# An FFT filter with two feed-forward layers on one core: weight lower parts formed by TensorE, the gate's half moved into the gain, the last inverse stage in fp32r

## The chip, the cores and the metric

The kernel runs on one core of one Trainium2 chip. The metric is the device time of one execution in microseconds (us), the median of several runs. One core has TensorE (PE, with its weight loads shown apart as PEld), VectorE (DVE), ScalarE (ACT), GpSimd (POOL) and SyncE (SP), and 16 DMA engines. All transfers but the early filter's stores are issued from SP's queue.

## The reference, cut to what matters

Sizes: batch 8, sequence 3072, width 256, so 24576 rows of 256; first layer 1024 wide, second 2048 wide.

```python
X = np.fft.rfft(x, axis=1)
Y = X * (filt_r + 1j * filt_i)[None]
x = np.fft.irfft(Y, n=3072, axis=1).reshape(24576, 256)

h = x @ w_in                                  # 256 -> 1024
solu = h * softmax(h)
ln = (solu - mean) / sqrt(var + 1e-6) * g_ln
x2 = ln @ w_out                               # 1024 -> 256

h = x2 @ w_in2                                # 256 -> 2048
g = h * (1 / (1 + exp(-1.702 * h)))
out = g @ w_out2                              # 2048 -> 256
```

The weights arrive as 8-byte floating-point words, and the kernel makes float32 values of them on the chip.

## The kernel before, in words

**Precision.** PE multiplies in two ways here. Operands of type fp32 go in whole, and the profile shows each such matmul as two records of weight load and matmul. Operands of type fp32r are split by the kernel into an upper part (`hi`, an ACT copy that rounds to fp32r) and a lower part (`lo`, a DVE or POOL subtraction), and a product is three matmuls: hi by hi, lo by hi, hi by lo (`product`, and the `terms` lists). Each fp32r matmul is one weight load and one matmul record.

**The filter.** The transform of 3072 points is done as 128 by 24. `step1` multiplies by the 128x128 matrix `fwd1` (fp32 for the first `direct` steps, else three fp32r terms), the result goes to `a_d` in device memory, 32 groups are transformed, weighted and transformed back (`forward`, `weigh`, `inverse`), and `store_z` puts them into `z_d`. Batch 0 is done alone by `EarlyFilter`, then batches 1 and 2 (`ahead`, `dense`), 3 and 4, and so on beside the layers.

**The layers.** There are 96 pairs of 128 rows. For each, class `First` loads `zr` from `z_d`, does the last inverse stage `y` (line 664): four combinations of a half of the width `c` and a piece `cut` of 128 rows, each one fp32 matmul with 128 weight columns out of `zr` and 128 moving columns out of `inv1`. Its result is split into `xh` and `xl`; then come `hidden`, the soft maximum and the normalization (`top` to `norm`), a transposition through device memory (`shuffle`, `gather`, `turn`), and `project`, whose sum `x2` is put into a tile with the tag `zr` (line 777) and split into `x2s`. Class `Second` takes two pairs at a time: 16 steps of `hidden` (line 839), `tanh`, `gate`, `split_hi`, `split_lo` and `output` (line 878), then `finish` (a DVE transposition into `ob`) and `store`. The tag `zr` has one buffer, which the load of `zr` and the sum `x2` use in turn.

**The weights.** Class `Weights` converts 24 parts of 128x512 words. Each goes through `magnitude` (ACT), `clamp`, `shift`, `sign`, `exponent`, `lower` and `add` (six DVE operations: lines 316, 322, 329, 334, 338, 343), `scale_rows` (ACT: the gain `g_ln` into `w_out`, or 0.5 into `w_out2`, line 352), `split_hi` (ACT, line 368) and `split_lo` (DVE, line 371). Parts 0 to 7 in the order of work are the first layer's, 8 to 23 the second layer's.

**Order.** The order on each engine is written out by hand: every step is entered with a due time (`at`), and the instructions are issued in the order of these times. One unit of the time is about 2.2 us in the steady part; a pair has 16 units. The tables `FIRST`, `SECOND`, `FILTER`, `DENSE` and `EARLY` hold the offsets. Each engine, and SP's queue, works through its own list in that order and waits where an operand isn't there.

```python
def product(out, w, x):
    for m, (i, j) in enumerate(((0, 0), (1, 0), (0, 1))):
        nc.tensor.matmul(out, w[i], x[j], start=m == 0, stop=m == 2)
```

Of the kernel before, what the change touches and what calls it, by code (L numbers as in the profile page):

```python
# [39 lines left out]
    "load": -19.18,  # L40
    "y": -15.41,
    "y_lo": -14.98,
    "hidden": ((-13.6, -11.48), (-3.67, -3.45)),
    "top": (-10.45, -2.27),
    "exp": (-9.62, -2.21),
    "weigh": (-8.86, -1.1),
    "square": (-8.1, 0.3),
    "norm": (-6.71, 0.45),
    "shuffle": (-6.64, 1.09),
    "gather": (-4.79, 2.67),  # L50
    "turn": (-1.22, 6.89),
    "u_hi": (-1.02, 7.3),
    "u_lo": (-0.4, 7.44),
    "project": ((9.08, 10.02), (11.05, 11.52)),
    "x2_add": (10.24, 12.96),
    "x2_hi": 13.25,
    "x2_lo": 13.63,
# [4 lines left out]
    "gate": 1.19,  # L62
    "split_hi": 2.49,
    "split_lo": 3.19,
    "output": 4.92,
    "finish": 5.15,
    "store": 6.9,
# [4 lines left out]
    "slots": (-0.44, 3.27, 3.36, 15.01),  # L72
    "first": (-5.28, -2.04, 0.2, 0.75),
    "second": (-4.86, -3.09, -2.5, 0.32, 1.88, 9.31, 12.49, 15.49, 15.68),
# [4 lines left out]
    "start": 15.65,  # L79
    "slots": (0.78, 4.28, 8.58, 12.36),  # L80
    "second": (-6.7, -3.27, -2.21, -0.12, 0.47, 5.53, 7.59, 10.86, 11.01),
# [6 lines left out]
    "end": -36.99,  # L88
    "step1": 25.97,
    "step2": 0.83,  # L90
    "gap": 6.0,
    "x": (-8.35, 0.03),
    "gt": (4.66, 5.2, -4.45),
    "first": (-1.3, -0.46, 5.21),
    "second": (-0.4, 0.64, 1.73, 1.99, 2.68, 3.25, 3.99, 4.34, 4.91),
    "more": (-2.73, -1.19, 0.91, 1.34),
    "direct": 20,
    "between": 0,
    "ahead": ((-20.99, -0.21), (1.01, 1.32)),
    "opening": (-0.05, 2.9),  # L100
    "shift": (-2.49, -2.3, -0.12),
    "loads": (-63.46, -85.07, -66.92, -63.78, -40.07, -39.95, -38.89, -39.87, -38.15, -36.42, -35.26, -29.67, -30.46, -26.83, -28.61, -26.9, -23.26, -23.0, -19.51, -21.51, -16.67, -16.56, -10.11, -9.34),
    "convert": (-61.36, -57.05, -48.5, -52.08, -39.08, -37.53, -36.03, -34.35, -33.55, -30.14, -29.23, -26.36, -27.59, -24.72, -22.78, -21.43, -19.42, -15.97, -16.78, -14.99, -11.07, -11.7, -6.6, -7.06),
    "weight": (-0.98, -0.23, 0.17, 0.46, 0.65, 1.06, 1.27, 1.37, 1.79, 2.41),
    "small": (-44.22, -37.8),
# [24 lines left out]
def dft_constants():  # L130
# [63 lines left out]
    dft1 = np.concatenate([fwd1, inv1], 1)  # L194
# [4 lines left out]
def fft_filter_solu_gelu(  # L199
# [42 lines left out]
    dma(out=dft1_sb, in_=dft1.rearrange("p (t n) -> p t n", t=2))  # L242
# [3 lines left out]
    inv1 = dft1_sb[:, 1]  # L246
# [7 lines left out]
    def load_gain(b):  # L254
        part, rows = blocks(g_ln, b)
        dma(out=g_sb[part], in_=rows.rearrange("(k f) -> f k", f=Q))

# [19 lines left out]
    class Weights:  # L277


        def __init__(self, n, dst, src, gain, k0, kn, c0, cn):  # L280
            self.dst = dst, slice(k0, k0 + kn), slice(c0, c0 + cn)
            self.shape = [P, kn, cn]
            k, c = slice(k0, k0 + kn), slice(c0, c0 + cn)
            self.half = dst is w4
# [34 lines left out]
        def shift(self):  # L319
            self.mag = p2.tile([P, 512], I32, tag="th", name="w_mag")  # L320
            self.f = self.mag.bitcast(F32)
            nc.vector.tensor_scalar(
                out=self.mag, in0=self.wt, scalar1=3, scalar2=0x3FFFFFFF,
                op0=ALU.logical_shift_left, op1=ALU.bitwise_and)

        def sign(self):

            self.top = p2.tile([P, 512], I32, tag="gh", name="w_top")
            nc.vector.scalar_tensor_tensor(
                out=self.top, in0=self.high, scalar=-0x40000000, in1=self.mag,  # L330
                op0=ALU.bitwise_and, op1=ALU.bitwise_or)
# [5 lines left out]
        def lower(self):  # L337
            nc.vector.scalar_tensor_tensor(
                out=self.f, in0=self.low, scalar=2.0 ** -52, in1=self.power,
                op0=ALU.mult, op1=ALU.mult)  # L340

        def add(self):
            nc.vector.tensor_tensor(self.f, self.f, self.top.bitcast(F32), op=ALU.add)
            self.f = self.f.rearrange("p (k n) -> p k n", k=self.shape[1])

        def scale_rows(self):
            if self.half:

                f, self.f = self.f, self.top.bitcast(F32).rearrange(
                    "p (k n) -> p k n", k=self.shape[1])  # L350
                for k in range(self.shape[1]):
# [4 lines left out]
            elif self.gain is not None:  # L356
                for k in range(self.shape[1]):
                    g = self.gain[:, self.k0 + k:self.k0 + k + 1]
                    nc.scalar.activation(
                        out=self.f[:, k], in_=self.f[:, k], func=AF.Copy, scale=g)  # L360

        def split_hi(self):
            dst, k, c = self.dst
            if not dst:
                t = p1.tile([P, 2, K2, D], F32R, tag="w4", name="w4")
                dst.extend(t[:, i] for i in range(2))
            self.hi, self.lo = (t[:, k, c] for t in dst)
            nc.scalar.copy(out=self.hi, in_=self.f)

        def split_lo(self):  # L370
            nc.vector.tensor_tensor(self.lo, self.f, self.hi, op=ALU.subtract)
# [277 lines left out]
    class First:  # L649
        def __init__(self, n):  # L650
            self.n = n
            self.h, self.e, self.v, self.e_d, self.ut, self.x2 = {}, {}, {}, {}, {}, {}

        def load(self):
            b, q = divmod(self.n, NPAIR)
            assert filtered[b] == NG
            self.cuts = segments(q * 2 * P, 2 * P)
            q0, q1 = self.cuts[0][0], self.cuts[-1][0] + 1
            self.zr = p1.tile([N1, 2, D], F32, tag="zr", name="zr")
# [30 lines left out]
        def top(self, a):  # L690
            nmx = p3.tile([P, 1], F32, tag="nmx", name="nmx")
# [3 lines left out]
        def exp(self, a):  # L695
            e = p2.tile([P, FF1], F32, tag="e", name="e")
            se = p3.tile([P, 1], F32, tag="se", name="se")
# [3 lines left out]
            q = p3.tile([P, 1], F32, tag="q", name="q")  # L701
# [5 lines left out]
        def weigh(self, a):  # L707

            e, q = self.e[a], self.v[a]
            su = p3.tile([P, 1], F32, tag="su", name="su")  # L710
            nc.vector.scalar_tensor_tensor(  # L711
                out=e, in0=self.h[a], scalar=1.0, in1=e, op0=ALU.mult, op1=ALU.mult, accum_out=su)
            nmu = p3.tile([P, 1], F32, tag="nmu", name="nmu")
# [4 lines left out]
        def square(self, a):  # L718
            e, (q, nmu) = self.e[a], self.v[a]
            ssq = p3.tile([P, 1], F32, tag="ssq", name="ssq")  # L720
# [4 lines left out]
            rs = p3.tile([P, 1], F32, tag="rs", name="rs")  # L725
# [65 lines left out]
    def plan_first(n):  # L791
# [6 lines left out]
        for a in range(2):  # L798
            in_order(
                v["load"], v["y"], v["y_lo"], *v["hidden"][a],  # L800
                *(v[step.__name__][a] for step in steps), *blocks, v["x2_add"][1], v["x2_hi"], v["x2_lo"], 14.0)
        at(r + v["load"], o.load)
        at(r + v["y"], o.y)
# [14 lines left out]
    class Second:  # L818
# [47 lines left out]
        def output(self, d):  # L866
# [6 lines left out]
            for j in range(self.nf):  # L873
                f = self.nf * d + j
                for h in range(2):
                    for m, (ww, gg) in enumerate(terms):
                        o = self.o[:, h] if self.nf == 1 else self.o[:, h, 0]
                        nc.tensor.matmul(  # L878
                            o, ww[:, f, h * P:(h + 1) * P], self.part(gg, j),
                            start=(f == 0 and m == 0), stop=(f == K2 - 1 and m == 2))  # L880

        def finish(self):

            self.ob = []
            for i in range(len(self.block)):
                pool, tag = ((p1, "ob"), (p2, "xs"))[i]
# [66 lines left out]
    for batches in together[2:]:  # L953
# [9 lines left out]
        plan_filter(batches, lambda i: [piece(i - 4) + d for d in FILTER["first"]], second)  # L963
    for w in weight_parts():
        i = w.n
        t = v["convert"][i]
        steps = (
            w.magnitude, w.clamp, w.shift, w.sign, w.exponent, w.lower, w.add, w.scale_rows,
            w.split_hi, w.split_lo)
        in_order(v["loads"][i], t + v["weight"][0])  # L970
        at(v["loads"][i], w.load)
        in_order(*v["weight"])
        for d, step in zip(v["weight"], steps, strict=True):
            at(t + d, step)
# [43 lines left out]
```

## Time and profile before

| | |
|---|---|
| median of 3 runs | 3665.89 us (3664.22 to 3667.66) |
| the profiled execution | 3660.58 us, span from first to last instruction 3658.7 us |
| mean granted TensorE clock | 0.986 |
| PE busy | 3564.5 us, 97% of the span |
| DVE, ACT, POOL busy | 75%, 56%, 23% |
| DMA | 434.90 MB, mean 119 GB/s |

A row of a group of instructions gives line, engine, operation, names of what is written and read, rows*columns of the weights and the shape of the moving operand, the count, then busy time in us, the mean of one in ns, and the idle time of the engine before it with what ended it. The granted clock is 1.00 at 2.4 GHz and 0.5 at 1.2 GHz. Matmuls are pipelined: a matmul's length holds the way through the array too, so what one costs in a row of many is the distance between starts and not the length.

### The profile page before, as it was taken

To read this page: it belongs to the slowest core of one execution; us is meant where nothing else is said; L and a number is where in the kernel's file an instruction comes from. 1 tells how busy PE (TensorE), PEld (TensorE's weight loads), DVE (VectorE), ACT (ScalarE), POOL (GpSimd) and SP (SyncE) were. 2 spreads that over 40 slices of the span, in tenths; PEclk is the share of its full clock that TensorE was granted. 3 is DMA by queue.
4 is the path that set the end of the run, shared out by engine and by line. 5 is a ranking of instruction groups with operands and counts; after the bars stand their busy time and mean duration, and the time that the engine had idled before them with its cause. 6 is when DMAs were issued, how large, how long until landed. Compare 5 with 4: busy or idle time off the path is not lost.

```text
span 3658.7 us, 50562 instructions
## 1 busy us (share of the span) xinstructions
PE 3564.5 (97%) x16768; PEld 2936.7 (80%) x16768; DVE 2751.7 (75%) x4005; ACT 2041.4 (56%) x3786; POOL 849.1 (23%) x1285
## 2 busy tenths in 40 slices
PE   6589999999999999999999999999999999999999
PEld 4277888888888888888888888888888888888887
DVE  4978887667888887667888787667777777676675
ACT  2556665555555555555656565555555564454453
POOL 0133332222222222232222222222222221111110
PEclk9689999999999999999999999999999999999999
DMA  9845653434444443443444444333333332222221
GB/s 278 259 135 144 166 136 121 129 118 115 118 118 123 119 119 107 134 125 107 118 124 119 117 119 118 117 102 107 108 109 108 106 106 80 81 75 82 78 79 29
DMA packets 388870, 434.90 MB, mean 119 GB/s; under 512 B 147328, under 2 KB 297984, under 8 KB 388608
## 3 DMA queue, kind: packets, MB, share of 16 engines
q1 hardware_dynamic: 383296, 425.38, 40.4%
q10 hardware_dynamic: 5312, 6.29, 0.5%
q8 instruction: 132, 2.16, 0.3%
q14 instruction: 130, 1.06, 0.1%
HBM read 233.31 MB, written 176.16 MB: 112 GB/s over the span
## 4 chain that ended last, share of the span: by engine, by line
PE 89%; DVE 3%; DMA 3%; ACT 2%; issue 1%; POOL 0%; SPq 0%; POOLq 0%; DVEq 0%; ACTq 0%
PE o L878 27%; PE h L839 27%; PE x L768 15%; PE h L686 13%; PE f L407 5%; PE yt L668 2%; DMA a_d<-az 1%; DVE gl L863 1%; DVE ob L889 0%; DMA zr<-z_d 0%; ACT h L722 0%; DMA wst<-in_w_in 0%; ACT th L846 0%; DVE nmx L692 0%; PE f L449 0%
## 5 line engine op out<-in xcount | busy, mean ns | idle before, releaser
L878 PE MATMUL o<-gh,w 128*128 128x512 f32 (+1 forms) x3136 | 963.3, 389 | 2.9 <-DVE ob L889 2.9
L839 PE MATMUL h<-x2s,w_hi 128*128 128x512 f32 (+1 forms) x3136 | 955.5, 387 | 0.0
L839 PEld LDWEIGHTS h<-x2s,w_hi 128*128 128x128 f32 x3136 | 577.5, 189 | 113.7 <-ACT x2s L786 0.4
L857 ACT CAST gh<-th 128x512 fp32r<-128x512 f32 x768 | 472.5, 615 | 336.4 <-DVE th L851 329.2
L878 PEld LDWEIGHTS o<-gh,w 128*128 128x128 f32 x3136 | 570.4, 189 | 110.7 <-issue 6.2
L863 DVE TENSOR_TENSOR gl<-th,gh 128x512 fp32r<-128x512 f32 x768 | 556.4, 725 | 131.8 <-ACT gh L857 117.3
L878 PE MATMUL o<-gl,w 128*128 128x512 f32 (+1 forms) x1568 | 606.4, 387 | 2.5 <-DVE gl L863 2.5
L846 ACT ACTIVATE th<-h 128x512 f32<-128x512 f32 x768 | 459.3, 598 | 239.3 <-PE h L839 237.7
L851 DVE SCALAR_TENSOR_TENSOR th<-th,h 128x512 f32<-128x512 f32 x768 | 522.2, 680 | 22.4 <-ACT th L846 21.1
L839 PE MATMUL h<-x2s,w_lo 128*128 128x512 f32 (+1 forms) x1568 | 478.1, 386 | 0.0
L780 DVE TENSOR_TENSOR x_sum<-x,x_sum 128x256 f32<-128x256 f32 x192 | 81.5, 425 | 513.7 <-ACT x_sum L779 513.7
L698 ACT ACTIVATE e<-h,nmx 128x1024 f32<-128x1024 f32 x192 | 214.6, 1118 | 410.5 <-DVE nmx L692 366.2
L768 PE MATMUL x<-u,w_hi 128*128 128x512 f32 x1536 | 384.5, 393 | 7.3 <-DVE u L759 6.1
L702 POOL TENSOR_SCALAR q<-se 128x1 f32<-128x1 f32 x192 | 45.4, 237 | 1423.3 <-ACT e L698 1423.1
L878 PEld LDWEIGHTS o<-gl,w 128*128 128x128 f32 x1568 | 294.6, 188 | 70.7 <-DVE gl L863 11.4
L768 PEld LDWEIGHTS x<-u,w_hi 128*128 128x128 f32 x1536 | 288.6, 189 | 73.3 <-DVE u L759 12.0
L839 PEld LDWEIGHTS h<-x2s,w_lo 128*128 128x128 f32 x1568 | 293.0, 188 | 61.6
L779 ACT COPY x_sum<-x 128x256 f32<-128x256 f32 x192 | 70.9, 369 | 373.0 <-PE x L768 373.0
L711 DVE SCALAR_TENSOR_TENSOR e<-h,e 128x1024 f32<-128x1024 f32 x192 | 234.0, 1219 | 19.9 <-ACT e L698 0.7
L686 PE MATMUL h<-w_hi,xh 128*128 128x512 f32 x768 | 240.9, 395 | 2.0 <-ACT xh L673 2.0
L748 DVE STREAM_TRANSPOSE ut<-e 128x1024 f32<-128x1024 f32 x192 | 237.0, 1234 | 6.5 <-DMA e<-e_d 6.4
L686 PE MATMUL h<-w_hi,xl 128*128 128x512 f32 x768 | 238.3, 392 | 0.1
(90 smaller groups left out, 5158.0 us busy)
## 6 DMA issues: line engine op xcount, KB each, us to landing
e_d<-e SPq DMA_DIRECT2D x192, 512.0 KB, 2.9
e<-e_d SPq DMA_DIRECT2D x768, 128.0 KB, 3.1
gt<-in_groups SPq DMA_DIRECT2D x144, 264.0 KB, 3.8
zr<-z_d SPq DMA_DIRECT2D x96, 256.0 KB, 3.0
out<-ob SPq DMA_DIRECT2D x768, 32.0 KB, 1.6
xin<-in_x SPq DMA_DIRECT2D x84, 256.0 KB, 3.5
a_d<-az SPq DMA_DIRECT2D x84, 256.0 KB, 2.4
bt<-a_d SPq DMA_DIRECT2D x96, 192.0 KB, 3.8
```

What stands on the lines that cost most here:

```text
L407: nc.tensor.matmul(out, w[i], x[j], start=m == 0, stop=m == 2)
L686: nc.tensor.matmul(hs, xx[:, c, a * P:(a + 1) * P], ww[:, c, f * 512:(f + 1) * 512], start=(m == 0 and c == 0), stop=(m == 2 and c == 1))
L698: nc.scalar.activation(out=e, in_=self.h[a], func=AF.Exp, bias=self.v[a], accum_out=se)
L711: nc.vector.scalar_tensor_tensor(out=e, in0=self.h[a], scalar=1.0, in1=e, op0=ALU.mult, op1=ALU.mult, accum_out=su)
L748: nc.vector.transpose(out=self.ut[a].rearrange("p k (i t) -> p k i t", t=Q), in_=self.e.pop(a).rearrange("p (i k f) -> p k i f", i=P // Q, ...
L768: nc.tensor.matmul(self.x2[c][:, :n].rearrange("p i t -> p (i t)"), w2[f][:, kk, c * P:(c + 1) * P], self.u[:, kk, :n].rearrange("p i a t ...
L839: nc.tensor.matmul(self.part(t, j), ww[:, c, f * P:(f + 1) * P], xx[..., c, :], start=(m == 0 and c == 0), stop=(m == 2 and c == 1))
L846: nc.scalar.activation(out=th, in_=self.t[d], func=AF.Tanh, scale=0.851)
L851: nc.vector.scalar_tensor_tensor(out=self.g[d], in0=self.g[d], scalar=1.0, in1=self.t.pop(d), op0=ALU.add, op1=ALU.mult)
L857: nc.scalar.copy(out=gh, in_=self.g[d])
L863: nc.vector.tensor_tensor(gl, th, gh, op=ALU.subtract)
L878: nc.tensor.matmul(o, ww[:, f, h * P:(h + 1) * P], self.part(gg, j), start=(f == 0 and m == 0), stop=(f == K2 - 1 and m == 2))
```

## The change

1. **Last inverse stage.** `zr` is split by a new ACT copy `z_hi` and a new DVE subtraction `z_lo` (in place), `inv1` is split once at the start, and `y` becomes three fp32r matmuls for each of its four combinations instead of one fp32 matmul.
2. **Lower parts of the second layer's weights.** For parts 8 to 23 (`by_pe`) `add` and `split_lo` fall away. PE forms top + small - hi with unit matrices (one fp32 and two fp32r matmuls of 512 columns, in a PSUM tile that shares the tag of `o`), and ACT copies the result into `lo`. The unit matrices are loaded and copied once, into the two buffers of the tag `fh`.
3. **The half.** The 0.5 of `w_out2` is put into `g_ln` by one ACT multiplication, the `tanh` scale is doubled, and the 16 ACT operations of line 352 fall away. `w4` is stored with its column order turned at the split.
4. **Buffers.** `ob` takes the tags `xs` and `zr` instead of `ob` and `xs`; the small statistics share one tile per half pair.
5. **Order.** All tables are new. Among them: `store` at 11.4 instead of 6.9, the load of `zr` at -19.66 instead of -19.18 with `z_hi` at -16.7 and `z_lo` at -16.41, `direct` 24 instead of 20, and the first steps of batches 1 and 2 spread over a longer stretch (`ahead`).

```diff
@@ tables
-    "load": -19.18,
-    "y": -15.41,
+    "load": -19.66,
+    "z": (-16.7, -16.41),
+    "y": -15.38,
...
-    "store": 6.9,
+    "store": 11.4,
...
-    "direct": 20,
+    "direct": 24,
...
-    "ahead": ((-20.99, -0.21), (1.01, 1.32)),
+    "ahead": ((-42.69, 5.82), (1.55, 1.76)),
...
+    "by_pe": 8,
+    "unit": -34.76,
@@ constants
-    inv1 = dft1_sb[:, 1]
+    inv1 = cst.tile([N1, 2, N1], F32R, name="inv1")
+    nc.scalar.copy(out=inv1[:, 0], in_=dft1_sb[:, 1])
+    nc.vector.tensor_tensor(inv1[:, 1], dft1_sb[:, 1], inv1[:, 0], op=ALU.subtract)
...
+    def load_unit():
+        t = p2.tile([P, 2, P], F32, tag="fh", name="unit_in")
+        dma(out=t, in_=dft1[:, 2 * N1:].rearrange("p (t n) -> p t n", t=2))
+        unit.append(p2.tile([P, 2, P], F32R, tag="fh", name="unit"))
+        nc.scalar.copy(out=unit[0], in_=t)
@@ class Weights
+            self.by_pe = gain is None and n >= EARLY["by_pe"]
...
+            if self.by_pe:
+                self.small = p2.tile([P, 512], F32R, tag="fl", name="w_small")
...
         def scale_rows(self):
-            if self.half:
...
-                    nc.scalar.activation(
-                        out=self.f[:, k].rearrange("p (h a c) -> p a h c", h=2, c=Q),
-                        in_=f[:, k].rearrange("p (a h c) -> p a h c", h=2, c=Q),
-                        func=AF.Copy, scale=0.5)
...
+                if not scaled:
+                    scaled.append(nc.scalar.mul(self.gain, self.gain, 0.5))
...
+        def total(self):
+            if not sums:
+                sums.append(ps_o.tile([P, 2, 512], F32, tag="o", name="w_lo"))
+            self.rest = sums[0][:, self.n % 2]
+            terms = (
+                (unit[0][:, 0].bitcast(F32), self.f), (unit[0][:, 0], self.small),
+                (unit[0][:, 1], self.hi))
+            for m, (w, t) in enumerate(terms):
+                nc.tensor.matmul(self.rest, w, t, start=m == 0, stop=m == 2)
+
+        def store_lo(self):
+            nc.scalar.copy(out=self.lo, in_=self.order(self.rest))
@@ class First
+        def z_hi(self):
+            self.zh = p1.tile([N1, 2, D], F32R, tag="zh", name="zh")
+            nc.scalar.copy(out=self.zh, in_=self.zr)
+
+        def z_lo(self):
+            nc.vector.tensor_tensor(self.zl, self.zr, self.zh, op=ALU.subtract)
...
                 for q, m, n, i in self.cuts:
-                    nc.tensor.matmul(
-                        self.yt[:, c, i:i + n],
-                        self.zr[:, q - self.cuts[0][0], c * P:(c + 1) * P], inv1[:, m:m + n],
-                        start=True, stop=True)
+                    z = [t[:, q - self.cuts[0][0], c * P:(c + 1) * P] for t in (self.zh, self.zl)]
+                    product(self.yt[:, c, i:i + n], z, [inv1[:, j, m:m + n] for j in range(2)])
@@ class Second
-            nc.scalar.activation(out=th, in_=self.t[d], func=AF.Tanh, scale=0.851)
+            nc.scalar.activation(out=th, in_=self.t[d], func=AF.Tanh, scale=1.702)
...
-                            o, ww[:, f, h * P:(h + 1) * P], self.part(gg, j),
+                            o, ww[:, h, f], self.part(gg, j),
...
-                pool, tag = ((p1, "ob"), (p2, "xs"))[i]
+                pool, tag = ((p2, "xs"), (p1, "zr"))[i]
@@ plan
+        if w.by_pe:
+            steps, offsets = (*steps, w.split_hi, w.total, w.store_lo), v["weight_pe"]
```

## Rows read from the trace of the kernel before

**Rows 1.** The page's part 1: busy time, share and instructions of each engine.
```profile
PE 3564.5 (97%) x16768; PEld 2936.7 (80%) x16768; DVE 2751.7 (75%) x4005; ACT 2041.4 (56%) x3786; POOL 849.1 (23%) x1285
```

**Rows 2.** The windows view: four stretches; length, busy us, granted clock, DMA share, GB/s.
```profile
90.00:200.00 110.00, 65.29 (x175) 36.17 (x175) 98.22 (x166) 62.90 (x118) 18.93 (x24) 0.72 0.79 243
200.00:280.00 80.00, 71.85 (x383) 60.66 (x383) 58.96 (x79) 42.96 (x79) 24.43 (x35) 0.90 0.49 139
280.00:3640.00 3360.00, 3354.09 (x15901) 2787.61 (x15900) 2543.58 (x3663) 1906.77 (x3530) 805.44 (x1222) 1.00 0.39 111
```

**Rows 3.** The page's part 4: the chain that ended last, by line.
```profile
PE o L878 27%; PE h L839 27%; PE x L768 15%; PE h L686 13%; PE f L407 5%; PE yt L668 2%; DMA a_d<-az 1%; DVE gl L863 1%; DVE ob L889 0%; DMA zr<-z_d 0%; ACT h L722 0%; DMA wst<-in_w_in 0%; ACT th L846 0%; DVE nmx L692 0%; PE f L449 0%
```

**Rows 4.** Timeline of PE, steady part: start us, us from first start to last end.
```profile
2002.15 0.62 PE L839 MATMUL h<-x2s,w_hi 128*128 128x512 f32 x2
2002.60 1.05 PE L668 MATMUL yt<-dft_sb,zr 128*128 128x128 f32 x8
2003.41 0.71 PE L878 MATMUL o<-gh,w 128*128 128x512 f32 x2
...
2022.62 0.61 PE L839 MATMUL h<-x2s,w_hi 128*128 128x512 f32 x2
2023.07 1.11 PE L768 MATMUL x<-u,w_lo 128*128 128x256 f32 x8
2024.03 0.63 PE L878 MATMUL o<-gh,w 128*128 128x512 f32 x2
```

**Rows 5.** Groups by line and form, whole span: matmuls and weight loads of PE.
```profile
L686 PE MATMUL h<-w_hi,xl 128*128 128x512 f32 x768 | 238.3, 392 | 0.1
L668 PE MATMUL yt<-dft_sb,zr 128*128 128x128 f32 x768 | 104.3, 280 | 5.6 <-DMA zr<-z_d 4.9 <-ACT az L453 0.7
L768 PEld LDWEIGHTS x<-u,w_lo 128*128 128x128 f32 x1536 | 210.6, 191 | 15.5
L407 PEld LDWEIGHTS f<-fh,mt 96*96 96x96 f32 x512 | 81.6, 162 | 27.1 <-ACT fh L401 0.3
```

**Rows 6.** Timeline of PE and PEld: a matmul after a pause, and weight loads before y.
```profile
661.07 0.50 PE L878 MATMUL o<-gl,w 128*128 128x512 f32 x1 [0.33 <-DVE gl L863]
661.07 0.19 PEld L878 LDWEIGHTS o<-gl,w 128*128 128x128 f32 x1 [0.75 <-DVE gl L863]
2002.38 1.08 PEld L668 LDWEIGHTS yt<-dft_sb,zr 128*128 128x128 f32 x8
```

**Rows 7.** Groups by form from 90 to 205 us: DVE, ACT and PE.
```profile
L343 DVE TENSOR_TENSOR w_mag<-w_mag,w_top 128x512 f32<-128x512 f32 x20 | 14.0, 699 | 0.4
L371 DVE TENSOR_TENSOR w_lo<-w_mag,w_hi 128x512 fp32r<-128x512 f32 x12 | 10.4, 866 | 0.8 <-ACT w_hi L368 0.8
L371 DVE TENSOR_TENSOR w<-w_top,w 128x512 fp32r<-128x512 f32 x8 | 5.5, 683 | 0.0
L352 ACT ACTIVATE w_top<-w_mag 128x256 f32<-128x256 f32 x16 | 5.8, 411 | 5.6 <-DVE w_mag L343 5.6
L449 PE MATMUL f<-xin,dft_sb 128*128 128x512 f32 x40 | 31.8, 905 | 34.0 <-DMA xin<-in_x 30.5 <-ACT w_hi L368 1.8 <-ACT az L453 1.7
```

**Rows 8.** Lines 786, 789 and 662: ns of one, min/median/max; the load's us to landing.
```profile
L786 ACT CAST x2s<-x_sum x96: 619/623/627, 190.5 to 3603.8; 128x512 fp32r<-128x512 f32 x96
L789 DVE TENSOR_TENSOR x2s<-x_sum,x2s x96: 677/694/1196, 191.2 to 3604.9; 128x512 fp32r<-128x512 f32 x96
DMA to landing us min/median/max: 2.6/3.0/7.7
```

**Rows 9.** Timeline of SP's queue: the load of zr for the y of 2002.60.
```profile
1996.97 0.34 SPq L662 DMA_DIRECT2D zr<-z_d  x1
```

**Rows 10.** Waits from 400 to 3600 us: us in total, times, longest; of PE.
```profile
PEld o L878 <- DVE gl L863: 10.7, 35, 0.7
```

More of the change, by code (lines that the diff above doesn't have):

```diff
@@ L87 @@
 EARLY = {
-    "end": -36.99,
-    "step1": 25.97,
+    "end": -36.94,
+    "step1": 33.21,
     "step2": 0.83,
[L91 to L96, printed above, removed]
-    "direct": 20,
-    "between": 0,
-    "ahead": ((-20.99, -0.21), (1.01, 1.32)),
[L100 to L105, printed above, removed]
+    "gap": 5.92,
+    "x": (-6.16, 0.78),
+    "gt": (11.33, 6.08, -3.87),
+    "first": (5.19, 13.75, 23.78),
+    "second": (-2.38, -0.82, 1.17, 1.35, 1.41, 2.24, 2.65, 3.46, 4.07),
+    "more": (-1.52, 0.41, 1.35, 3.29),
+    "direct": 24,
+    "between": 0,
+    "ahead": ((-42.69, 5.82), (1.55, 1.76)),
+    "opening": (-0.02, 2.96),
+    "shift": (-2.36, -2.36, -0.34),
+    "loads": (-63.81, -95.0, -70.72, -68.47, -42.5, -41.19, -41.01, -39.0, -37.7, -40.54, -32.78, -32.38, -29.5, -30.46, -25.3, -27.58, -21.84, -19.81, -19.09, -17.15, -16.57, -14.95, -10.51, -10.23),
+    "convert": (-62.2, -59.01, -42.22, -52.05, -38.93, -37.02, -35.32, -34.19, -31.92, -31.26, -29.92, -27.97, -26.86, -24.09, -22.59, -21.49, -19.19, -15.43, -15.56, -14.4, -8.59, -12.4, -5.51, -6.84),
+    "weight": (-0.96, -0.01, 0.27, 0.65, 0.72, 1.25, 1.34, 1.94, 2.15, 2.97),
+    "weight_pe": (-1.11, -0.32, -0.07, 0.17, 0.42, 0.46, 0.83, 1.74, 2.17),
+    "by_pe": 8,
+    "unit": -34.76,
+    "small": (-45.1, -39.49),
 }
@@ L344, in add @@
[L344 removed]
+            nc.vector.tensor_tensor(self.f, self.f, self.power, op=ALU.add)
         def scale_rows(self):
[L347 to L356 removed]
+            if self.gain is not None:
+                if not scaled:
+                    scaled.append(nc.scalar.mul(self.gain, self.gain, 0.5))
@@ L357, in scale_rows @@
                 for k in range(self.shape[1]):
                     g = self.gain[:, self.k0 + k:self.k0 + k + 1]
-                    nc.scalar.activation(
-                        out=self.f[:, k], in_=self.f[:, k], func=AF.Copy, scale=g)
+                    f = self.f[:, k * D:(k + 1) * D]
+                    nc.scalar.activation(out=f, in_=f, func=AF.Copy, scale=g)
         def split_hi(self):
[L363 to L366, printed above, removed]
@@ L367, in split_hi @@
-            self.hi, self.lo = (t[:, k, c] for t in dst)
-            nc.scalar.copy(out=self.hi, in_=self.f)
-        def split_lo(self):
-            nc.vector.tensor_tensor(self.lo, self.f, self.hi, op=ALU.subtract)
+            if self.dst is w4:
+                if not w4:
+                    t = p1.tile([P, 2, 2, K2, P], F32R, tag="w4", name="w4")
+                    w4.extend(t[:, i] for i in range(2))
+                k = slice(self.k0, self.k0 + self.shape[1])
+                self.hi, self.lo = (
+                    t[:, :, k].rearrange("p h k (a c) -> p (k a) h c", c=Q) for t in w4)
+                self.order = lambda t: t.rearrange("p (m h c) -> p m h c", h=2, c=Q)
+            else:
+                k, c = self.part
+                self.hi, self.lo = (t[:, k, c] for t in self.dst)
+                self.order = lambda t: t.rearrange("p (k n) -> p k n", k=self.shape[1])
@@ new lines, in split_hi @@
+            nc.scalar.copy(out=self.hi, in_=self.order(self.f))
+        def split_lo(self):
+            nc.vector.tensor_tensor(self.lo, self.order(self.f), self.hi, op=ALU.subtract)
+        def total(self):
[7 more added lines that the diff above has]
+                nc.tensor.matmul(self.rest, w, t, start=m == 0, stop=m == 2)
@@ L799, in plan_first @@
             in_order(
-                v["load"], v["y"], v["y_lo"], *v["hidden"][a],
+                v["load"], *v["z"], v["y"], v["y_lo"], *v["hidden"][a],
                 *(v[step.__name__][a] for step in steps), *blocks, v["x2_add"][1], v["x2_hi"], v["x2_lo"], 14.0)
         at(r + v["load"], o.load)
+        at(r + v["z"][0], o.z_hi)
+        at(r + v["z"][1], o.z_lo)
         at(r + v["y"], o.y)
@@ L966, in fft_filter_solu_gelu @@
         t = v["convert"][i]
[L967 to L970, printed above, removed]
-        at(v["loads"][i], w.load)
-        in_order(*v["weight"])
-        for d, step in zip(v["weight"], steps, strict=True):
+        steps = (w.magnitude, w.clamp, w.shift, w.sign, w.exponent, w.lower)
+        if w.by_pe:
+            steps, offsets = (*steps, w.split_hi, w.total, w.store_lo), v["weight_pe"]
+        else:
+            steps, offsets = (
+                *steps, w.add, w.scale_rows, w.split_hi, w.split_lo), v["weight"]
+        in_order(v["loads"][i], t + offsets[0])
+        at(v["loads"][i], w.load)
+        in_order(*offsets[:6], *offsets[7 if w.by_pe else 6:])
+        in_order(offsets[3], *offsets[6:])
+        if w.gain is not None:
+            in_order(v["small"][0], t + offsets[7])
+        for d, step in zip(offsets, steps, strict=True):
             at(t + d, step)
```

92 lines of the change are left out of this document (47 added, 45 removed).

## The prediction

> **What bounds the kernel now.** I read the busy shares first: PE 97% of the span, DVE 75%, ACT 56% [rows 1]. The chain that ended last says the same: its largest parts are PE's lines 878, 839, 768 and 686, and the stage that is changed, line 668, is in it with 2% [rows 3]. Since a share hides stages, I then cut the span into stretches [rows 2]. From 280 to 3640 us PE is busy 3354.09 of 3360 us at a granted clock of 1.00, so each us of PE's own work added there lengthens the run, and work of DVE, ACT or SP there costs nothing while it keeps ahead. From 90 to 200 us it is otherwise: DVE is busy 98.22 of 110 us, PE 65.29, the clock is 0.72, the DMA share 0.79. That is the stretch of the weights, and there it is DVE work that counts.
>
> **Last inverse stage, PE.** In the steady part the eight records of `y` start at 2002.60 and end 1.05 us later; with 0.28 us for one [rows 5] the last starts 0.77 us after the first, so 0.77 / 7 = 0.111 us apart, and 8 x 0.111 = 0.89 us for a pair [rows 4]. The change makes 12 fp32r matmuls of 128 columns of them. No row of before shows an fp32r matmul that narrow, so I bound it by the nearest. Of 256 columns, eight take 2024.03 - 2023.07 = 0.96 us, 0.120 each; of 512, two take 0.45 us, 0.227 each [rows 4]. The difference is 0.107 us for 256 columns, 0.418 ns a column, one at 2.4 GHz. By the columns alone 128 would take 0.120 - 0.0535 = 0.0665 us: the lower end.
>
> But each of the twelve needs a weight load of its own, 128 columns, and the rows show what one costs when nothing covers it. After a pause the load and its matmul are shown starting together at 661.07, and the matmul is 0.50 us long [rows 6] where the same shape has 0.392 in a stream [rows 5]: 0.11 us longer. Load lengths agree: 191 ns for 128 columns, 162 for 96, so 0.91 ns a column [rows 5], some 0.11 us for 128. And a load does not run further ahead than one matmul: the first of `y` starts at 2002.38 [rows 6], when the second of the two matmuls that began at 2002.15 does (2002.15 + 0.227) [rows 4]. So a load begins when the matmul before begins, and its own matmul can't begin before some 0.11 us are over. At 256 columns that is just covered by the streaming; at 128 it isn't. I take 0.111 us a matmul, the distance that the eight loads of `y` have now; upper end 0.120, the distance at 256 columns, since a shorter one shouldn't take longer. So 12 x 0.111 = 1.33 us for a pair, and 1.33 - 0.89 = +0.44 us; for 96 pairs **+42.6 us** (upper end 12 x 0.120 - 0.89 = 0.55, +53 us; lower end 12 x 0.0665 - 0.89 = -0.09, -9 us, which is the first rival). PE has no idle time to hide it in.
>
> The Trainium skill speaks against this step: "TensorE: Matmul & The Clock Gate", section "Back-to-back issue gap", gives about 81 ns a matmul for a stream of loads and matmuls of 128 columns. By it the stage would take 0.97 us, +8 us in all, instead of +42.6. No row of before shows such a stream in fp32r; the 0.11 us after a pause is the reason why I don't follow it.
>
> **Last inverse stage, ACT, DVE and the load.** `z_hi` is an ACT copy like line 786, 0.623 us, `z_lo` a DVE subtraction like line 789, 0.694 us [rows 8]: 60 us of ACT and 67 us of DVE over the run. They lie beside PE (DVE goes from 2543.58 to about 2605 of 3360 us [rows 2]). In the chain of one pair they stand between the landing of `zr` and `y`. The load is issued at 1996.97 [rows 9], lands after 3.0 us [rows 8], and `y` starts at 2002.60 [rows 4]: 2.6 us of slack for 1.32 us of work. `z_hi` waits on ACT for that transfer; behind it stand the `tanh` and the `gh` copies for PE's line 878. PE's largest wait from 400 to 3600 us is 10.7 us in 35 times [rows 10], so there is room. I take +2 us, from 0 to +48 (half a us late in each pair, if that cover is gone).
>
> **Weights.** For 16 parts one `add`, 0.699, and one `split_lo`, 0.683 (0.866 the mean of the twelve with three long ones), fall from DVE [rows 7]: 16 x 1.38 = 22 us. Three `z_lo` come into the stretch, 2 us. DVE has 98.22 us of 110 [rows 2], so at most 20 us of the stretch can go by DVE, a few more if the six long subtractions and pauses go with it (26). DMA stands in the way: PE waits 30.5 us for x there [rows 7] at a share of 0.79 [rows 2]; the new order moves part of the x loads behind the stretch, where the share is 0.49. Against it stands PE's new work: an fp32 matmul of 512 columns is two records of twice 512 columns, 4 x 512 x 0.418 ns = 0.86 us, and two fp32r ones 0.45 us: 1.31 us, 21 us for 16 parts, in the 44.7 us that PE is idle there. At the lower level of the clock (0.905 us a record of such a matmul [rows 7]) it is 16 x 2.67 = 43 us, all of the idle time; then PE takes DVE's place and nothing is won. `store_lo` is another ACT copy of 512 columns, 16 x 0.62 us [rows 8] for line 352's 16 x 0.411 us [rows 7], and ACT has room (62.90 of 110 [rows 2]). I take **-14 us**, from -26 to +5.
>
> **The rest.** `direct` 24: four steps with one fp32 matmul (0.86 us) for three fp32r ones (0.68), +0.7 us. The half in the gain, the `tanh` scale, the order of `w4` and the common statistics tile change no operation on PE and none that is late: 0. `ob` in the tag `zr` is written when `y` has read it; its 16 stores now stand 4.5 units (10 us) later in SP's list, and the next to want the buffer is ACT's copy of `x2`, three units after. I put it at 0; if that copy waits it is in the upper end below.
>
> **Sum.** 42.6 - 14 + 2 + 0.7 = +31 us on the profiled execution's 3660.6 (span 3658.7): 3692. The profiled execution lies 5.3 us under the median of the three runs, so on that scale 3666 + 31 = 3697 us.
>
> **Rivals.** (1) *The weight loads do not hold the narrow matmuls.* If a load may begin before the matmul ahead of it, the twelve go by their columns, 0.0665 us: -9 - 14 + 3 = -20, 3646 us, faster. It decides at the distance p where 12p - 0.89 makes up for 11 us in 96 pairs: p = 0.084 us. For it: two loads in a row never show what a shorter matmul would allow. Against it: [rows 6]. Half covered, at 0.089 us, it is +17 - 11 = +6, 3672, about no change. Chance 16%, some 9% of it the fast end. (By the Trainium skill's 81 ns, in "TensorE: Matmul & The Clock Gate", section "Back-to-back issue gap", it would be 3663; the trace neither shows nor excludes it.) (2) *Narrow fp32r is carried out as fp32*, 24 records of 0.111: 2.66 us, +170 us, 3825 us. Nothing below 256 columns shows that it is not so; but 256 columns go as one record at full rate. 7%. (3) *The added waits come through*: `z_hi` on the load, or `x2` on the stores out of `zr`, half a us in most pairs: 3697 + 30 to 48, up to 3745 us; 10%. (4) *The stretch of the weights gives much more than DVE's share* and outweighs `y`: 42.6 us would be needed of 110; 4%, faster. (5) *By PE nothing is won* in the stretch: 3711 us, inside the forecast's own range.
>
> **How the numbers follow.** The forecast (0.111 to 0.120 us, -26 to 0 for the weights) has 63%: 3685 to 3722. The range reaches down over the half-covered cases of rival 1, to a distance of 0.070 us, and up over most of rival 3: 3650 to 3740, leaving out the fast end of (1), (2) and (4). A measurement of this kernel can tell about 0.2%, 7 us, from no change. Faster: 9% of (1) and 4% of (4), 0.13. Same: the rest of (1) and the lowest corner of the forecast, 0.09. Slower: 0.78.
>
> **What would show it.** In the changed kernel's timeline the twelve records of `y` should span about 1.33 us from the first to the next line's matmul; 0.8 means rival 1, 2.7 rival 2. PE should be at 1.00 and full from 280 us on, with no new wait before line 668. `hidden` of the second layer should begin some 14 us earlier than now, DVE's `add` and `split_lo` should stand there 8 times each, not 24. The forecast is wrong if `y` does not grow, or if the early stretch shrinks by over 35 us.

## The result, and the profile after

The changed kernel takes 3709.58 us (median; 3708.22 to 3711.27), the kernel before 3666.77 us in the same comparison (3664.22 to 3669.94): 1.0117 times as long, 95% interval 1.0099 to 1.0134. It is 43 us slower. The forecast was 31 us slower, 3697 us, in a range of 3650 to 3740.

The page of the changed kernel, part 1 and the head of part 4, beside [rows 1, 3]: PE's busy share has gone from 97% to 98% of a longer span, and in the chain PE has 79% where it had 89%, and more of ACT and DVE appears, the new `z_lo` (line 698) among it. First the head of part 4 before, then the changed kernel:

```profile
PE 89%; DVE 3%; DMA 3%; ACT 2%; issue 1%; POOL 0%; SPq 0%; POOLq 0%; DVEq 0%; ACTq 0%
```

```profile
PE 3629.2 (98%) x17212; PEld 2984.9 (80%) x17212; DVE 2784.0 (75%) x4070; ACT 2136.5 (58%) x3881; POOL 733.9 (20%) x1281
...
PE 79%; ACT 6%; DVE 5%; issue 2%; DMA 1%; SPq 0%; POOL 0%; DVEq 0%; POOLq 0%; ACTq 0%
PE o L915 24%; PE h L876 24%; PE x L803 14%; PE h L720 10%; PE f L435 4%; PE yt L435 3%; ACT e L733 1%; DVE stats L727 1%; ACT th L883 1%; ACT u L791 1%; DVE th L888 1%; DMA e<-e_d 1%; DVE x2s L824 1%; DVE zr L698 1%; ACT x2s L821 1%
```

The windows view of the changed kernel, with the columns of [rows 2]. In the stretch of the weights DVE has gone from 98.22 to 84.28 us, PE from 65.29 to 82.79, and the clock from 0.72 to 0.88. From 280 us on PE is almost as full as before (3350.08 of 3360 us for 3354.09).

```profile
90.00:200.00 110.00, 82.79 (x283) 49.44 (x284) 84.28 (x145) 66.78 (x122) 7.84 (x20) 0.88 0.79 248
200.00:280.00 80.00, 71.34 (x381) 58.42 (x380) 60.95 (x82) 47.91 (x87) 24.43 (x37) 0.96 0.50 140
280.00:3640.00 3360.00, 3350.08 (x15970) 2780.66 (x15971) 2562.53 (x3706) 1972.46 (x3578) 701.36 (x1219) 1.00 0.39 110
```

The last inverse stage in the steady part, timeline of PE, to be held against [rows 4]. (Its matmuls have the line of `product`, 435, and the names `zh` and `zr` for the two halves of what was loaded.)

```profile
2021.63 0.62 PE L876 MATMUL h<-x2s,w_hi 128*128 128x512 f32 x2
2022.09 0.22 PE L435 MATMUL yt<-inv,zh 128*128 128x128 f32 x1
2022.15 0.28 PE L435 MATMUL yt<-inv,zr 128*128 128x128 f32 x1
...
2023.16 0.27 PE L435 MATMUL yt<-inv,zr 128*128 128x128 f32 x1
2023.27 0.28 PE L435 MATMUL yt<-inv,zh 128*128 128x128 f32 x1
2023.38 0.68 PE L915 MATMUL o<-gh,w 128*128 128x512 f32 x2
```

From the first of the twelve to the last are 2023.27 - 2022.09 = 1.18 us; the eight records before had 0.77. With the distance behind the last one the stage takes 1.3 us where it took 0.9.

**Where the time went, pair by pair.** The start of this stage in each of the 96 pairs is a clock that both traces have. Against the kernel before, pair 4 starts 8.2 us earlier (258.9 for 267.1), so the early part has gained. From there the changed kernel loses: pair 60 starts 23.9 us later (2353.8 for 2329.9), pair 95 49.2 us later (3594.1 for 3544.8). That is 57.4 us in 91 pairs, 0.63 a pair, of which the twelve matmuls explain 0.44, 40 us. Some 17 us are something else. (The profiled execution of before lies 6 us under its median, so on medians the whole is 43 and not 50 us.)

### The profile page after: what moved, and what is told of

The parts are those of the page before. It is cut to its first block, busy times and chain, and to the rows that moved or that the text cites. A ratio compares the mean times of both kernels' runs of the same rounds, so it can differ in the third digit from the quotient of the medians.

```text
span 3708.5 us, 51353 instructions
## 1 busy us (share of the span) xinstructions
PE 3629.2 (98%) x17212; PEld 2984.9 (80%) x17212; DVE 2784.0 (75%) x4070; ACT 2136.5 (58%) x3881; POOL 733.9 (20%) x1281
## 4 chain that ended last, share of the span: by engine, by line
PE 79%; ACT 6%; DVE 5%; issue 2%; DMA 1%; SPq 0%; POOL 0%; DVEq 0%; POOLq 0%; ACTq 0%
PE o L915 24%; PE h L876 24%; PE x L803 14%; PE h L720 10%; PE f L435 4%; PE yt L435 3%; ACT e L733 1%; DVE stats L727 1%; ACT th L883 1%; ACT u L791 1%; DVE th L888 1%; DMA e<-e_d 1%; DVE x2s L824 1%; DVE zr L698 1%; ACT x2s L821 1%
## 5 line engine op out<-in xcount | busy, mean ns | idle before, releaser
L915 PEld LDWEIGHTS o<-gh,w 128*128 128x128 f32 x3136 | 578.4, 188 | 114.1 <-issue 2.1
L733 ACT ACTIVATE e<-h,stats 128x1024 f32<-128x1024 f32 x192 | 214.5, 1117 | 351.7 <-DVE stats L727 338.2
L727 DVE TENSOR_REDUCE stats<-h 128x1 f32<-128x1024 f32 x192 | 235.1, 1225 | 154.4 <-PE h L720 154.4
L803 PEld LDWEIGHTS x<-u,w_hi 128*128 128x128 f32 x1536 | 283.5, 189 | 75.8 <-DVE u L794 18.7
L737 POOL TENSOR_SCALAR stats<-stats 128x1 f32<-128x1 f32 x192 | 44.8, 233 | 1449.1 <-ACT e L733 1449.0
L430 POOL TENSOR_TENSOR fl<-bt,fh 96x512 fp32r<-96x512 f32 (+1 forms) x128 | 162.3, 1268 | 579.6 <-ACT fh L429 579.2
L757 ACT ACTIVATE h<-e,stats 128x1024 f32<-128x1024 f32 x192 | 215.4, 1122 | 57.4 <-POOL stats L749 57.3
```

The source lines that it names most:

```text
L727: nc.vector.tensor_reduce(out=nmx, in_=self.h[a], op=ALU.max, axis=AX.X, negate=True)
L733: nc.scalar.activation(out=e, in_=self.h[a], func=AF.Exp, bias=self.v[a], accum_out=se)
L803: nc.tensor.matmul(self.x2[c][:, :n].rearrange("p i t -> p (i t)"), w2[f][:, kk, c * P:(c + 1) * P], self.u[:, kk, :n].rearrange("p i a t ...
L915: nc.tensor.matmul(o, ww[:, h, f], self.part(gg, j), start=(f == 0 and m == 0), stop=(f == K2 - 1 and m == 2))
```

## The experiments

All kernels are the changed kernel with the edit shown, but for the seventh, which starts from the kernel before; the eighth to tenth have the first one's edit beside their own. Times are medians.

**1. The stage set back to fp32.**

```diff
-                    z = [t[:, q - self.cuts[0][0], c * P:(c + 1) * P] for t in (self.zh, self.zl)]
-                    product(self.yt[:, c, i:i + n], z, [inv1[:, j, m:m + n] for j in range(2)])
+                    nc.tensor.matmul(
+                        self.yt[:, c, i:i + n],
+                        self.zr[:, q - self.cuts[0][0], c * P:(c + 1) * P], inv1[:, m:m + n],
+                        start=True, stop=True)
...
-        at(r + v["z"][0], o.z_hi)
-        at(r + v["z"][1], o.z_lo)
```

> The changed kernel with the last inverse stage as before: one fp32 matmul for each of the four combinations, no z_hi and z_lo; all else stays as changed. My theory: the stage's 12 narrow fp32r matmuls cost 12 x 0.111 us against 8 x 0.111 (42.6 us in 96 pairs), and a further 14 us are waits inside the stage for z_lo. Then both go: 3709.6 - 42.6 - 14 = 3653 us, under the kernel before by the early stretch's gain of about 10 us. Rival, order and buffers (ob in the tag zr, new tables) cause the waits: only 43 us go, 3667 us, no different from before.

Measured: 3654.13 us (3651.87 to 3655.05), 0.9971 of before (0.9958 to 0.9983). 55 us have gone, 1 us from what the theory gave, and the rest of the change is faster than the kernel before. So the loss lies in this stage, and it is more than the 43 us forecast for the matmuls; the rival, by which only 43 us go, is out.

**2. Half of the columns.**

```diff
-                    product(self.yt[:, c, i:i + n], z, [inv1[:, j, m:m + n] for j in range(2)])
+                    for k, (w, j) in enumerate(((0, 0), (1, 0), (0, 1))):
+                        w_n = n if k == 0 else n // 2
+                        nc.tensor.matmul(
+                            self.yt[:, c, i:i + w_n], z[w], inv1[:, j, m:m + w_n],
+                            start=k == 0, stop=k == 2, skip_group_check=True)
```

> The changed kernel with 64 instead of 128 moving columns in the second and third of each three matmuls of the last inverse stage (the lower terms are left out for half of the columns, so the output isn't the reference's). If the weight load holds these matmuls, their starts stay 0.111 us apart and the time stays at 3709.6 us within 4. If they are held by their columns, 8 x 64 x 0.418 ns = 0.21 us go in each pair, 21 us in all: 3689 us.

Measured: 3709.72 us (3706.92 to 3713.55), the changed kernel's time to 0.2 us. Timeline of PE, same stage:

```profile
2024.01 0.22 PE L707 MATMUL yt<-inv,zh 128*128 128x128 f32 x1
2024.06 0.24 PE L707 MATMUL yt<-inv,zr 128*128 128x64 f32 x1
2024.14 0.42 PE L707 MATMUL yt<-inv,zh 128*128 128x64 f32 x2
2024.40 0.24 PE L707 MATMUL yt<-inv,zr 128*128 128x64 f32 x1
2024.48 0.42 PE L707 MATMUL yt<-inv,zh 128*128 128x64 f32 x2
2024.73 0.24 PE L707 MATMUL yt<-inv,zr 128*128 128x64 f32 x1
```

The `zr` matmuls come at 2024.06, 2024.40 and 2024.73: three matmuls take 0.33 to 0.34 us, 3 x 0.111 as with full columns, although two of the three stream half as much. (Within a triple the starts are shown unevenly, so I go by the distance from one `zr` matmul to the next.) So the columns don't hold these matmuls. What holds them is something that each has once, whatever its columns, and the weight load of 0.11 us that the prediction read from [rows 5] and [rows 6] fits in size. A fixed cost of the same length that isn't the load is not excluded: all loads of this stage have 128 columns in every run.

**3. DVE's work put back.**

```diff
             nc.vector.scalar_tensor_tensor(
                 out=self.small, in0=self.low, scalar=2.0 ** -52, in1=self.power,
                 op0=ALU.mult, op1=ALU.mult)
+            if self.by_pe:
+                for _ in range(2):
+                    nc.vector.tensor_tensor(self.power, self.power, self.power, op=ALU.max)
```

> The changed kernel with two idle DVE operations of 128x512 after lower in each of the 16 parts whose lower half PE forms: the DVE work that the change took away is put back, with nothing else changed (the values are unused). My theory, that the early stretch is shorter because DVE is relieved: the last inverse stage of pair 4 starts at 267 to 272 us instead of 258.9, and the whole is 3718 to 3723 us. Rival, the gain comes from the new order of the x loads or from the clock that PE's new work keeps up: pair 4 stays within 2 us, 3710 us.

Measured: 3729.68 us (3729.24 to 3730.17), 20 us more than the changed kernel. Pair 4 starts its stage at 278.7 us instead of 258.9, and the distance to the changed kernel stays at 19 to 21 us from there to the end, so the rival (pair 4 within 2 us) is out. The windows view of this kernel for the same stretch: DVE is back at 95.94 us, PE falls to 73.64 us (207 matmuls in the stretch where the changed kernel has 283), and the clock to 0.81.

```profile
90.00:200.00 110.00, 73.64 (x207) 40.67 (x207) 95.94 (x165) 56.42 (x104) 7.87 (x15) 0.81 0.67 209
```

It follows that time added to DVE in this stretch costs nearly its full length: 32 operations of 0.69 us, 22 us of busy time, cost 20. The effect was larger than I expected (8 to 13 us), because I counted only with the gain that the changed kernel shows as a whole.

**4. One of PE's three terms.**

```diff
-            for m, (w, t) in enumerate(terms):
-                nc.tensor.matmul(self.rest, w, t, start=m == 0, stop=m == 2)
+            nc.tensor.matmul(self.rest, *terms[1], start=True, stop=True)
```

> The changed kernel with one of the three matmuls that form a lower part: only the fp32r one of the small words (the other two terms are left out, so the lower parts are wrong in their last bits and the output isn't quite the reference's). It takes 16 x (0.86 + 0.23) = 17 us of PE at the full clock out of the early stretch. My theory, that this work lies in PE's idle time there: pair 4 starts its last inverse stage within 3 us of 258.9, the whole is 3706 to 3710 us. Rival, it stands in the way of the first pairs: pair 4 is 5 to 10 us earlier, 3700 to 3704 us.

Measured: 3713.71 us (3712.3 to 3715.54), pair 4 at 261.8 us: within the 3 us of my theory, but the whole is 4 us above its range. Taking 17 us of PE's work away gains nothing; it is 4 us slower than the changed kernel. The windows view shows one thing that goes with it, the granted clock, 0.74 instead of 0.88. That the lower clock is the cause of the 4 us is not shown.

```profile
90.00:200.00 110.00, 73.22 (x221) 44.87 (x220) 85.61 (x149) 66.59 (x122) 7.23 (x20) 0.74 0.78 246
```

**5. The stage later in PE's order.**

```diff
-    "y": -15.38,
-    "y_lo": -14.98,
+    "y": -14.75,
+    "y_lo": -14.35,
```

> The changed kernel with the last inverse stage 0.63 units (1.4 us) later in PE's order, y at -14.75 and y_lo at -14.35. My theory, that PE stands inside the stage until z_lo is written: its 12 starts span 1.18 us in the late pairs too (now 1.45 and 1.63), and 10 to 14 us go: 3696 to 3700 us. Rival, the wait only moves to the next step (xh, hidden): 3710 us.

Measured: 3765.2 us (3760.18 to 3768.78), 56 us slower than the changed kernel, a miss for both. The stage itself did close up: 1.18 us from first to last in the late pairs. But the next step, `hidden` of the first layer, now stands too close behind and waits for `xl`. Waits of this kernel from 400 to 3600 us:

```profile
PEld h L720 <- DVE xl L711: 72.3, 60, 2.0
...
PE h L720 <- DVE xl L711: 46.0, 52, 1.5
```

Among the longest waits of the changed kernel there is none for `xl`. So moving the stage alone takes the wait for `z_lo` out of it and puts a larger one, for `xl`, into the next step. The rival had the place right and the size wrong.

**6. The stage with `z_lo` wanted last.**

```diff
-            for c in range(2):
-                for q, m, n, i in self.cuts:
-                    z = [t[:, q - self.cuts[0][0], c * P:(c + 1) * P] for t in (self.zh, self.zl)]
-                    product(self.yt[:, c, i:i + n], z, [inv1[:, j, m:m + n] for j in range(2)])
+            todo = [
+                (t, j, c, *cut) for pairs in (((self.zh, 0), (self.zh, 1)), ((self.zl, 0),))
+                for c in range(2) for cut in self.cuts for t, j in pairs]
+            for k, (t, j, c, q, m, n, i) in enumerate(todo):
+                nc.tensor.matmul(
+                    self.yt[:, c, i:i + n],
+                    t[:, q - self.cuts[0][0], c * P:(c + 1) * P], inv1[:, j, m:m + n],
+                    start=k == 0, stop=k == len(todo) - 1, skip_group_check=True)
```

> The changed kernel with the twelve matmuls of the last inverse stage in another order: the eight that need only z_hi first, the four with z_lo last. z_lo is then wanted 0.8 us after the stage begins and not after 0.1. My theory, that the steady part's added waits are for z_lo: the twelve span 1.18 to 1.25 us in the late pairs, 10 to 14 us go: 3696 to 3700 us. Rival, they come from elsewhere or only move to xh: 3706 to 3710 us.

Measured: 3694.35 us (3693.57 to 3698.41), 15 us less, a little more than the theory's 10 to 14. Timelines of PE, pair 84, first the changed kernel, then this one:

```profile
3212.73 0.22 PE L435 MATMUL yt<-inv,zh 128*128 128x128 f32 x1
3213.19 0.33 PE L435 MATMUL yt<-inv,zr 128*128 128x128 f32 x1 [0.24 <-DVE zr L698]
...
3214.36 0.28 PE L435 MATMUL yt<-inv,zh 128*128 128x128 f32 x1
```

```profile
3206.34 1.00 PE L706 MATMUL yt<-inv,zh 128*128 128x128 f32 x8
3207.18 0.61 PE L706 MATMUL yt<-inv,zr 128*128 128x128 f32 x4
3207.62 0.67 PE L919 MATMUL o<-gh,w 128*128 128x512 f32 x2
```

In the changed kernel the first matmul starts, and the second stands until `z_lo` is written: 3214.36 - 3212.73 = 1.63 us from first to last. With the order changed nothing is waited for, and the stage is at 0.84 + 0.44 = 1.28 us to the next line. Over pairs 4 to 95 the excess over 1.18 us in the changed kernel's stage adds up to 14.2 us, 11.6 of them from pair 64 on; here it adds up to 0.1. That is what the order gives back: against the changed kernel, pair 60 starts 0.5 us earlier and pair 95 11.5 us.

The changed kernel's timelines of SP's queue, ACT and DVE show why. The load is issued at 3207.01 and lands 2.7 us later, at 3209.7. `z_hi` starts only at 3211.79, 2.1 us after that, behind another ACT copy and without a pause; `z_lo` starts at 3212.45 after waiting for it, and PE arrives at 3212.73, while `z_lo` is still running. In none of the pairs 4 to 95 does ACT stand idle before `z_hi`: it waits for its place in ACT's list, and not for the transfer.

```profile
3207.01 0.34 SPq L691 DMA_DIRECT2D zr<-z_d  x1
```

```profile
3210.86 1.04 ACT L791 CAST u<-ut 128x1024 fp32r<-128x1024 f32 x1
3211.79 0.62 ACT L695 CAST zh<-zr 128x512 fp32r<-128x512 f32 x1
```

```profile
3212.45 0.69 DVE L698 TENSOR_TENSOR zr<-zr,zh 128x512 fp32r<-128x512 f32 x1 [0.62 <-ACT zh L695]
```

This kernel and the first experiment's differ in the stage alone, and in neither does PE stand inside it: 3694.35 - 3654.13 = 40 us for 96 pairs, 0.42 a pair. That is the price of twelve fp32r matmuls for eight fp32 records, which was forecast as 42.6.

**7. The stage alone, in the kernel before.** The kernel before takes the changed `load`, `z_hi`, `z_lo` and `y` and, to have the room, the common statistics tile and the tags of `ob`.

```diff
+    "z": (-16.7, -16.41),
     "y": -15.41,
...
-    "store": 6.9,
+    "store": 11.4,
...
-                pool, tag = ((p1, "ob"), (p2, "xs"))[i]
+                pool, tag = ((p2, "xs"), (p1, "zr"))[i]
```

> The kernel before with one part of the change alone: the last inverse stage in fp32r with z_hi and z_lo, and what makes room for it (common statistics tile, ob in the tags xs and zr, store at 11.4). Weights and all other tables stay as before. My theory: 12 x 0.111 for 8 x 0.111 us in 96 pairs is 42.6 us, waits for z_lo some 10 to 15 more since the tables give it no more room than in the changed kernel, and no gain in the early stretch: 3664 + 53 to 58 = 3717 to 3722 us, above the changed kernel. Rival, the waits come from the new tables and not from the stage: 3664 + 43 = 3707 us.

Measured: 3759.5 us (3758.8 to 3763.03), 1.0258 of before: 95 us, not 53 to 58. The direction was right, the size wrong. The changed tables had made more room for the new steps than I thought. Waits of this kernel from 400 to 3600 us: the stage waits for `z_lo` in twice as many pairs as the changed kernel (84 times for 35 at the weight load), and ACT waits for stores and transfers: its line `e` is shown behind `out` for 51.2 us in 26 times, where the kernel before has 19.7 in 10. Why `e` has to wait for stores is not shown.

```profile
ACT e L708 <- DMA out<-ob: 51.2, 26, 2.0
...
PEld yt L410 <- DVE zr L673: 38.7, 84, 1.0
...
PE yt L410 <- DVE zr L673: 18.0, 69, 0.9
```

The measure of the sixth experiment accounts for most of the rest: over pairs 4 to 95 the stage's excess over 1.18 us adds up to 44.9 us here, where the changed kernel has 14.2. With some 40 for the matmuls that leaves about 10 of the 95 us open. (By pairs, 13 us have gone when pair 4 starts.)

**8. The stage in fp32, and both `ob` and `store` as before.**

```diff
-    "store": 11.4,
+    "store": 6.9,
...
-                pool, tag = ((p2, "xs"), (p1, "zr"))[i]
+                pool, tag = ((p1, "ob"), (p2, "xs"))[i]
```

> The changed kernel with the last inverse stage as before (fp32), and also ob in its own tag and xs, and store at 6.9, as before: what is left of the change is the weights by PE, the half in the gain and the tables. If ob in the tag zr costs nothing on PE's path: 3654 us, as with the stage alone set back. Rival, ACT's waits for the stores out of zr (58 us in the changed kernel) reach PE: 3640 to 3648 us.

Measured: 3897.76 us (3894.09 to 3899.5), 1.0632 of before. Neither theory had this. Two more kernels tell the two lines apart.

**9. The same with `ob` alone set back.**

```diff
-                pool, tag = ((p2, "xs"), (p1, "zr"))[i]
+                pool, tag = ((p1, "ob"), (p2, "xs"))[i]
```

> The changed kernel with the last inverse stage in fp32 as before and ob in its own tag and xs as before, store left at 11.4. In the run with both ob and store set back the stores stand in SP's list ahead of the gathers of the second half pair, and PE waits for what comes out of them. If the place of the store is the cause, this kernel runs as the one with the stage alone set back: 3654 us, or up to 5 us under it if the tag zr cost anything. If the buffers are the cause, it is near 3890 us.

Measured: 3646.51 us (3644.66 to 3648.98), 0.995 of before (0.9937 to 0.9964), 7.6 us under the first experiment. It is the fastest of these kernels: weights by PE, the half in the gain and the new tables, without the fp32r stage. The tags of `ob` did cost something. In the first experiment's kernel ACT's copy of `x2` waits 12 times for stores from 400 to 3600 us, 41.6 us in all, and here never. (The edit moves both tiles of `ob`; the waits name the one in `zr`.)

**10. The same with `store` alone set back.**

```diff
-    "store": 11.4,
+    "store": 6.9,
```

> The changed kernel with the last inverse stage in fp32 as before and store at 6.9 as before, ob left in the tags xs and zr. If the place of the store in SP's list is the cause of the 243 us that were lost with both set back: 3870 to 3910 us. If the buffers are: 3654 us.

Measured: 3904.13 us (3902.76 to 3905.5). So it is the place of the store. SP's queue in this kernel, and its waits from 400 to 3600 us:

```profile
2000.61 0.34 SPq L772 DMA_DIRECT2D e_d<-e  x1
2001.89 8.25 SPq L935 DMA_DIRECT2D out<-ob  x16
2010.18 1.85 SPq L778 DMA_DIRECT2D e<-e_d  x4
```

```profile
DVE ut L782 <- DMA e<-e_d: 164.2, 41, 5.5
...
PEld o L912 <- DVE gl L897: 161.5, 43, 5.7
PE o L912 <- DVE gl L897: 143.3, 43, 5.3
```

Sixteen stores hold the queue for 8.25 us between a `shuffle` and its `gather`. The gathered rows are late, DVE's `turn` waits for them, and behind it in DVE's order stands `gl`, which PE's output needs. With `store` at 11.4 the gather (4.12 in these tables) stands ahead of the stores. In the kernel before, with `store` at 6.9 too, the gather has 2.67 in the tables and stands just ahead of the stores in SP's queue, and DVE's `turn` waits only 3.6 us for its rows from 400 to 3600 us. So it is the later gather of the new tables that makes the old place of the store costly. SP's queue before:

```profile
1969.54 0.34 SPq L738 DMA_DIRECT2D e_d<-e  x1
...
1972.59 2.61 SPq L744 DMA_DIRECT2D e<-e_d  x4
1975.30 7.50 SPq L901 DMA_DIRECT2D out<-ob  x16
```

## Why the prediction was right, and which terms were off

**The stage's matmuls: right.** 12 x 0.111 for 8 x 0.111 was forecast as 1.33 us for 0.89; from the second start at 2022.15 to the twelfth at 2023.27 there are ten distances of 0.112 us (the first start is shown only 0.06 us before the second, so I leave it out), and the stage takes 1.3 us. As time of the kernel it is 40 us (sixth against first experiment) for a forecast of 42.6. That the columns don't hold is shown by the half columns: the time didn't move. Rivals 1 and 2 fall with it. That it is the load that holds still rests on the 0.11 us of [rows 5] and [rows 6]; no run loads fewer weight columns. The Trainium skill's 81 ns for a stream of loads and matmuls of 128 columns ("TensorE: Matmul & The Clock Gate", "Back-to-back issue gap") does not hold for this fp32r stream; the measured 111 ns decides.

**The weights: right in kind and nearly in size.** -14 us was forecast, between -26 and +5. The ninth experiment, which has the weights and the tables but neither the stage nor the tag, is 18.7 us under before (3665.22 to 3646.51), and putting DVE's operations back costs 20. PE's new work was put at 21 us at the full clock and 43 at the lower level; in the changed kernel it is busy with these 64 matmuls for 28.4 us, at a mean granted clock of 0.88 (windows view of line 396, PE's time):

```profile
90.00:205.00 115.00, 28.38 (x64) 12.09 (x64) 0.88 0.76 240
```

That it lies in PE's idle time fits the fourth experiment, where taking most of it away gained nothing; but the clock fell with it, to 0.74, so that run alone doesn't prove it. Of the signs that were named, DVE's `add` and `split_lo` do stand there 8 times each. `hidden` of the second layer begins at 185.0 us for 191.2, 6 us earlier and not 14; in the ninth experiment's kernel it is 9. (The lower end of -26 was counted with six long subtractions; the trace of before has two, of 1.76 and 1.78 us.)

**The added steps of the stage: mis-sized.** I took +2 us, and 14 to 15 were measured (14.2 by the trace, 15 by the sixth experiment). The step that failed is the wait of `z_hi`. I let it begin when the transfer lands, and held 1.32 us of work against 2.6 us between landing and `y`. In the changed kernel it begins 2.2 us after the landing (median of pairs 4 to 63), because ACT works through its list until then. The two steps are then over some 3.5 us after the landing. Up to pair 63 PE comes to the stage 3.8 us after the landing, since the load was also put earlier, and mostly waits for nothing. From pair 64 on it comes after 3.1 us: pairs are 36 us apart there and not 37, while one batch is left in the filter (matmuls of 96x256 for 96x512, from 2497 us), and the stage stretches to 1.46 us, and to 1.63 us after the filter's last matmul at 3081 us. The landing itself was on time, and the slack in the late pairs of before, 2.1 us, would not have shown the loss: ACT's list had to be read as well. Rival 3 named a late `z_hi`, but with the load as the cause and half a us in most pairs.

**`ob` in the tag `zr`: mis-sized.** I put it at 0 and left it to the upper end; by the difference of the first and ninth experiments `ob`'s new tags cost 7.6 us. In the changed kernel's waits from 400 to 3600 us ACT stands before the `x2` copy for the stores:

```profile
ACT x_sum L814 <- DMA out<-ob: 53.6, 15, 5.8
```

**The sum.** Forecast +42.6 - 14 + 2 + 0.7 + 0 = +31. Measured, from kernel to kernel: -18.7 for weights and tables (before to the ninth), +7.6 for the tags of `ob` (to the first), +40 for the matmuls (to the sixth), +15 for `z_lo` (to the changed kernel): +44, beside +43 in the direct comparison, where before was 1.5 us slower than beside the ninth. The mechanism that decided, the stage's matmuls on a full PE, was forecast and is shown. That the total came within 13 us of the forecast is in part luck: two terms came out some 20 us higher than I took them, and the weights and the matmuls 7 to 8 lower.

What stays open: the early part gains 13 us at pair 4 in the ninth experiment, while putting DVE's work back costs 20 at the same place. Whether the new order, PE's new work or ACT's copies take the difference, or whether DVE's relief is worth less than its return costs, wasn't tried apart.

## What to carry to other kernels

Whether a split into three fp32r terms pays depends on the width of the moving side. At 512 columns the prediction's sums from the rows give 0.68 us for 0.86 (an estimate, which no run here tests alone). At 128 columns with 128 columns of weights for each matmul, count matmuls with their loads and not columns: 12 lost against 8. When an operand is split in two on two engines, let the matmuls that need only the first half go first, which gave back 15 us here without moving any step. The slack of such a split runs from its place in the list of the engine that does it, and not from the landing of its data. And where one queue issues everything, a batch of small stores is an operation with a length (8.25 us for 16), so look at what stands behind it before it is moved.

## What the hardware showed that I had not expected

The distance of the narrow fp32r matmuls didn't move at all when their columns were halved: 0.111 us each with 128 and, on the mean of three, with 128, 64 and 64. And more PE work in the stretch from 90 to 200 us came with a higher mean granted clock (0.88 with the three terms, 0.74 with one, 0.72 before, which also has other tables). From 90 to 205 us an fp32 record of 512 columns of the same step took 690 ns in the mean, where it took 905 before [rows 7]:

```profile
L477 PE MATMUL f<-xin,dft_sb 128*128 128x512 f32 x48 | 29.1, 690 | 15.2 <-DMA xin<-in_x 15.2
```
